# Softmax scaling and copies on another engine, weight conversion in whole pieces, and tables loaded elsewhere, in a fused attention, Fourier-mixing and feed-forward kernel

## The chip, the core and the metric

The kernel runs on one core of a Trainium2 chip. The core has five engines that each work through a list of instructions of their own, in order: TensorE (PE in the profile; PEld is its weight load), VectorE (DVE), ScalarE (ACT), GpSimd (POOL) and SyncE (SP), which here issues all the DMAs. The metric is the device time of one execution in microseconds. Before the change it is 2252.2 us, the median of three runs (2251.06 to 2255.11).

## What is computed

The reference is attention with normalised q and k, then a real part of a two-dimensional Fourier transform added to the result, then a normalised feed-forward block. There are 8 batches of 448 tokens, 12 heads of 64, so a model width of 768, and a hidden width of 3072. Everything is float32.

```python
rms = np.sqrt(np.mean(x * x, axis=-1, keepdims=True) + 1e-06)   # q and k: x / rms * g
scores = 1.0 / np.sqrt(64) * np.matmul(q_n, k_n.transpose(0, 1, 3, 2))
attn = np.exp(scores - np.max(scores, axis=-1, keepdims=True))
attn = attn / (np.sum(attn, axis=-1, keepdims=True) + 1e-09)
x = np.matmul(attn, v)                      # then heads side by side: (8, 448, 768)
mixed = np.real(np.fft.fft(np.fft.fft(x, axis=1), axis=2))
u = x + mixed
un = (u - mean(u)) / np.sqrt(var(u) + 1e-06)
out = u + np.maximum(un @ w_ch1, 0.0) @ w_ch2
```

The feed-forward weights come as float64 and are handed to the chip as pairs of 32-bit words.

## The kernel before

One batch goes through `attention`, `spectral` and `ffn`. The feed-forward part of batch b (`ffn(b)`) is interleaved by `merge` with attention and spectral part of batch b + 1 (`aux(b + 1)`), by costs that the generators yield. `aux(0)` has no feed-forward beside it: it is the start of the program. The code's order is a first wish; the compiler's scheduler then chooses the order on each engine from its own estimate, so what stands where is shown below from the built program.

**Attention** works on pairs of heads, six in a batch. `norm_pair` squares q and k, reduces to `ss`, raises to the power -0.5 on POOL (lines 239, `ss`), and multiplies; `gneg` is the product of the two norms' factors, loaded by `load_gains`. `transpose_pair` brings q and k into `QT` and `KD` (and `KL`, a remainder term). `softmax_pair` takes four row blocks c of 112 tokens: PE makes scores `S` for both heads, DVE takes the row extreme `mn`, ACT does the exponential into `P` and its row sum into `sm`, DVE adds 1e-9 to `sm` and takes the reciprocal, and then each half of `P` is scaled by it. In the first two batches (`EARLY = 2`) the first half is scaled on ACT and the second on DVE; later both are scaled on DVE. `value_pair` transposes `P` on PE into `pt`, copies it out to `T` and multiplies by v into `av`. In batch 0 (plain pairs, line 382) three of a pair's six copies `T` run on DVE and three on ACT. `fold` adds and subtracts halves of the attention output `xT` on DVE (`eo`, `sd`, `tot`).

**The spectral part** multiplies the folded halves by the tables `D1` and `D2` (`y`, `Y`, `ab`), which `load_dft` loads at the start, `D2` through a staging tile `d2s` of 113 rows that ACT copies and DVE subtracts from. Then it adds x (`u`), takes means and writes `u` to a DRAM buffer.

**The feed-forward part** has 24 `up` steps (18 matmuls into `h`, line 844) and 36 `down` steps (12 matmuls into `o`, line 865) per batch. Each product is three float32r passes with a high and a low part.

**Conversion.** In the first batch each of the 24 + 36 weight tiles is converted from 64-bit words by `convert` (line 632): a load into `dbl` (tag X, 4 slots), two ACT operations (lines 643, 644), three DVE operations (645, 649, 653), a POOL add (657), an ACT cast (658) and a POOL subtraction (659). A tile is done in two halves (line 688): 128x384 for a tile of w1, 128x256 for one of w2. The working tile `mag` (tag M) has two slots, each stream `W1`, `W2` three finished tiles. Converted tiles are also stored to DRAM, and later batches load them from there. `CONVERT_EARLY` spreads the first 14 tiles over `aux(0)`; names of those end in `e` (`magw1e`). The other 46 are converted during `ffn(0)`. `behind` ties each conversion instruction, during the start, to the fourth-last recorded one of its engine.

Most DVE, ACT and POOL work goes through a recording helper, so it shows line 111 (112 after the change); it is told apart by tile names.

Of the kernel before, what the change touches and what calls it, by code (L numbers as in the profile page):

```python
# [22 lines left out]
C = 112  # L23
# [64 lines left out]
def spectral_block(ctx, tc, q, k, v, g_q, g_k, w1, w2, d1, d2, out, nb=B):  # L88
# [54 lines left out]

    SLOTS = {"P": 8, "PT": 6, "X": 4, "M": 2, "unT": 6, "h": 6}

    def slot(tag, name, dtype=F32):
        return sb.tile([128, 900], dtype, tag=tag, name=name, bufs=SLOTS[tag])

    def sub(o, a, b_):
# [10 lines left out]

    KL = cpool.tile([128, 2, S], F32R, name="KL")
    G.memset(KL.bitcast(F32), 0.0)
# [162 lines left out]
    def softmax_pair(b, p, Pc):  # L325
        QT, KD, _ = ready[b, p]
        for c in range(NC):
            P = slot("P", f"P{b}_{p}_{c}")[:C, : 2 * S]
            Ph = [P[:, :S], P[:, S:]]
            mn = sb.tile([C, 2], F32, tag="mn", name=f"mn{b}_{p}_{c}", bufs=4)  # L330
            sm = sb.tile([C, 2], F32, tag="sm", name=f"sm{b}_{p}_{c}", bufs=4)
            cs = slice(c * C, (c + 1) * C)
# [34 lines left out]
            Pc.append(P)  # L367
            yield 760

    def value_pair(b, p, Pc, xT):  # L370
# [6 lines left out]
        if plain(b, p):  # L377
# [92 lines left out]
    rstds = {}  # L470

    def fold(b, p, xT, EO):

# [158 lines left out]
    def convert(src, bits, part, name):  # L632
# [30 lines left out]
    class Stream:  # L663
# [18 lines left out]
        def converted(self, i, name):  # L682
            hl = self.tile(name)
            src = self.doubles(i)
            bits = slot("M", f"mag{self.tag}{name}", U32)[:, : self.n * 128].rearrange(
                "r (c f) -> r c f", c=self.n
            )
            for c in (slice(0, self.n // 2), slice(self.n // 2, self.n)):
                convert(
                    src[:, c], bits[:, c], [hl[:, k, c] for k in range(2)],  # L690
                    f"{self.tag}{name}_{c.start}",
                )
            nc.sync.dma_start(self.kept(i), hl.bitcast(F32))
            return hl
# [205 lines left out]
    def warm():  # L900
# [45 lines left out]
```

## Time and profile before

| | before |
|---|---|
| median of the timed runs | 2252.2 us (2251.06 to 2255.11) |
| the profiled execution | 2245.9 us, span 2244.1 us |
| PE busy | 2107.8 us (94%) |
| DVE busy | 1636.7 us (73%) |
| ACT busy | 1074.1 us (48%) |
| POOL busy | 574.0 us (26%) |
| mean granted TensorE clock | 0.963 of full speed |

A share over the whole span is a mean over very different stages: in the first half millisecond of the span PE has gaps and the other engines are fuller, behind it PE has almost none. So the table by stage below is the one to start from. In all rows a time is in us unless it is marked as ns; the number in brackets behind a busy time counts instructions; what stands behind `<-` in square brackets is what ended the idle time ahead of an instruction. Durations of neighbouring instructions on one engine overlap a little, so the distance of two starts is what an instruction costs its engine in a row of them.

### The profile page before, as it was taken

How to read it: one execution, taken by the hardware profiler on the slowest of the kernel's cores; microseconds unless marked ns; L12 is line 12 of the kernel's file. 1: busy time of each engine (PE TensorE's matmuls, PEld its weight loads, DVE VectorE, ACT ScalarE, POOL GpSimd, SP SyncE). 2: the span in 40 equal slices, each digit the busy share in tenths (PEclk: the TensorE clock that was granted, in tenths of full speed). 3: DMA queues.
4: the chain of work that ended last, by engine and by line, in shares of the span. 5: the costliest groups of instructions: out<-in, count | busy, mean ns of one | idle time of the engine just before them, and what ended most of it. 6: DMA issues, size and time to landing. Idle time of an engine off the chain costs nothing.

```text
span 2244.1 us, 32060 instructions
## 1 busy us (share of the span) xinstructions
PE 2107.8 (94%) x11164; PEld 1851.1 (82%) x11164; DVE 1636.7 (73%) x3281; ACT 1074.1 (48%) x2452; POOL 574.0 (26%) x442
## 2 busy tenths in 40 slices
PE   6967986788999999999999999999999999999997
PEld 3336865667999999999999999999999999998997
DVE  6897899898688577876788587866788587753122
ACT  5856777475554255534554355524554355422100
POOL 5883567476122011210122021211121022000000
PEclk7997987899999999999999999999999999999999
DMA  5556555577755585556655575557655674539665
GB/s 137 174 167 210 171 171 163 173 266 256 218 174 169 184 238 165 180 182 207 200 171 177 193 222 169 173 177 225 187 171 177 207 215 161 177 132 279 212 215 136
DMA packets 299187, 425.37 MB, mean 190 GB/s; under 512 B 187489, under 2 KB 225362, under 8 KB 299026
## 3 DMA queue, kind: packets, MB, share of 16 engines
q1 hardware_dynamic: 299026, 423.32, 61.1%
q8 instruction: 89, 1.46, 0.3%
q14 instruction: 72, 0.59, 0.1%
HBM read 363.47 MB, written 65.27 MB: 191 GB/s over the span
## 4 chain that ended last, share of the span: by engine, by line
PE 76%; DVE 10%; issue 4%; DMA 3%; POOL 3%; ACT 2%; SPq 0%; DVEq 0%; POOLq 0%; ACTq 0%
PE h L844 28%; PE o L865 27%; PE S L342 5%; PE av L429 4%; PE pt L417 4%; PE y L520 1%; PE qk L305 1%; DVE magw L653 1%; DVE mn L111 1%; DMA dblw<-w 1%; POOL magw L657 1%; DVE magw L645 1%; PE oT L810 1%; DMA u_dram<-u 1%; DMA w<-w 1%
## 5 line engine op out<-in xcount | busy, mean ns | idle before, releaser
L865 PE MATMUL o<-hs,w 128*128 128x448 f32 x3456 | 801.0, 374 | 13.3 <-ACT w L658 4.4
L844 PE MATMUL h<-unT,w 128*128 128x448 f32 x3456 | 781.4, 371 | 3.3 <-DVE hs L111 3.3
L865 PEld LDWEIGHTS o<-hs,w 128*128 128x128 f32 x3456 | 643.9, 191 | 71.7 <-ACT w L658 5.8
L844 PEld LDWEIGHTS h<-unT,w 128*128 128x128 f32 x3456 | 640.5, 189 | 57.1 <-DVE hs L111 4.3
L111 ACT ACTIVATE P<-S,mn 112x448 f32<-112x448 f32 x384 | 243.1, 635 | 218.7 <-DVE mn L111 196.8
L111 POOL TENSOR_TENSOR qkn<-raw 112x1024 f32<-112x1024 f32 x47 | 90.4, 1924 | 740.4 <-PE qk L305 481.2
L111 DVE TENSOR_REDUCE mn<-S 112x1 f32<-112x448 f32 x384 | 232.9, 616 | 48.8 <-PE S L342 45.7
L111 ACT ACTIVATE hs<-h 128x448 fp32r<-128x448 f32 x192 | 104.4, 544 | 294.0 <-PE h L844 293.1
L111 DVE TENSOR_TENSOR acc<-o,acc 128x448 f32<-128x448 f32 x240 | 148.6, 620 | 106.9 <-PE o L865 105.2
L111 DVE SCALAR_TENSOR_TENSOR hs<-h,hs 128x448 fp32r<-128x448 f32 x192 | 119.2, 621 | 125.8 <-ACT hs L111 123.8
L429 PE MATMUL av<-T,vhl 128*128 128x448 f32 x504 | 181.5, 392 | 19.2 <-DVE T L111 12.5
L111 ACT CAST T<-pt 128x448 fp32r<-128x448 f32 x252 | 133.2, 532 | 133.9 <-PE pt L417 131.6
L111 DVE TENSOR_TENSOR T<-pt,T 128x448 fp32r<-128x448 f32 x252 | 154.9, 616 | 35.5 <-ACT T L111 34.0
L111 POOL TENSOR_TENSOR ss<-ss,nhalf 112x16 f32<-112x16 f32 x48 | 151.7, 3160 | 108.9 <-DVE ss L111 107.2
L111 DVE TENSOR_SCALAR P<-P,sm 112x448 f32<-112x448 f32 x336 | 159.5, 509 | 4.3
L342 PE MATMUL S<-KD,QT 128*112 128x448 f32 x352 | 142.6, 407 | 10.5 <-ACT P L111 5.2
L417 PE MATMUL pt<-ident,P 112*128 112x112 f32 x1008 | 147.0, 264 | 4.4 <-DVE R L111 2.8
L417 PEld LDWEIGHTS pt<-ident,P 112*128 112x128 f32 x1008 | 123.0, 143 | 25.7 <-DVE R L111 3.6
L111 POOL TENSOR_TENSOR rstd<-st,nhalf 112x1 f32<-112x1 f32 (+2 forms) x32 | 18.4, 575 | 487.5 <-DVE st L111 484.6
L342 PE MATMUL S<-KL,QT 128*112 128x448 f32 x352 | 134.7, 385 | 2.0 <-DVE KL L111 1.9
L429 PEld LDWEIGHTS av<-T,vhl 128*128 128x128 f32 x504 | 96.4, 192 | 32.0 <-DVE T L111 17.0
L657 POOL TENSOR_TENSOR magw<-magw,dblw 128x256 uint32<-128x256 uint32 (+1 forms) x92 | 87.4, 960 | 81.6 <-DVE magw L653 55.7
(121 smaller groups left out, 2680.3 us busy)
## 6 DMA issues: line engine op xcount, KB each, us to landing
w<-w SPq DMA_DIRECT2D x288, 512.0 KB, 4.3
w<-w SPq DMA_DIRECT2D x192, 768.0 KB, 4.5
dblw<-w SPq DMA_DIRECT2D x60, 256.0 KB, 3.0
dblw<-w SPq DMA_DIRECT2D x32, 384.0 KB, 3.9
raw<-q SPq DMA_DIRECT2D x96, 112.0 KB, 4.6
raw<-k SPq DMA_DIRECT2D x96, 112.0 KB, 3.7
v<-v SPq DMA_DIRECT2D x96, 96.0 KB, 3.6
u_dram<-u SPq DMA_DIRECT2D x24, 336.0 KB, 3.5
```

Source lines behind the costliest of these rows:

```text
L111: ins = emit(*args, **kwargs)
L305: nc.tensor.transpose(pt[:, c * C : (c + 1) * C], qk[:, i, c].rearrange("t h d -> t (h d)"), ident[:C, :C],)
L342: nc.tensor.matmul(s_, QT[:, h, cs], K[:, h], start=step == 0, stop=step == 1)
L417: nc.tensor.transpose(pt[:, c * C : (c + 1) * C], Pc[c][:, 512 * h + j * 128 : 512 * h + (j + 1) * 128], ident[:C, :C],)
L429: nc.tensor.matmul(av[:, :S], lv, T[:, i], start=(j == 0 and i == 0), stop=False)
L520: nc.tensor.matmul(o, src[:, par, t0 : t0 + n], D1[:, ri, par, cols], start=i != 1, stop=i != 0,)
L645: behind(nc.vector.tensor_scalar(out=value, in0=value, scalar1=MIN_HIGH, scalar2=MAX_HIGH, op0=ALU.max, op1=ALU.min,))
L653: behind(nc.vector.scalar_tensor_tensor(out=bits, in0=high, scalar=0xC0000000, in1=bits, op0=ALU.bitwise_and, op1=ALU.bitwise_or,))
L657: behind(nc.gpsimd.tensor_tensor(out=bits, in0=bits, in1=low, op=ALU.add))
L810: nc.tensor.transpose(op[:n, j * 128 : (j + 1) * 128], accs[b][:, 3 * half + j, t0 : t0 + n], ident,)
L844: pace(nc.tensor.matmul(o, w[:, a, c], unT[c][:, z], start=n == 0, stop=n == 17))
L865: pace(nc.tensor.matmul(o, w[:, a, f], hs[4 * g + f][:, z], start=n == 0, stop=n == 11))
```

## The change

Six things are edited.

1. In the first two batches both halves of `P` are scaled on ACT. In batch 0 the row sums of two row blocks are taken together (one addition and one reciprocal for four columns), in later batches those of all four (eight columns), and the scalings follow in a row.
2. In batch 0 all six copies `T` of a pair run on ACT.
3. `convert` takes a whole tile at once: 128x768 or 128x512. Tag X has two slots of double width. `fold` uses them in later batches.
4. `load_gains` stands ahead of the first pair's loads in the code.
5. `load_dft` is called at step 40 of `aux(0)` and no more after its first step; its second table comes in two DMAs, of 112 rows and of one row.
6. `KL` and `D2` share one tile, `rounded`.

```diff
     def softmax_pair(b, p, Pc):
         QT, KD, _ = ready[b, p]
+        together = 2 if b == 0 else NC
         for c in range(NC):
...
-            V.tensor_scalar(
-                out=sm, in0=sm, scalar1=1e-9, scalar2=None, op0=ALU.add
-            )
-            V.reciprocal(sm, sm)
-            for h in range(2):
-                if b < EARLY and h == 0:
-                    A.activation(Ph[h], Ph[h], AF.Copy, scale=sm[:, h : h + 1])
-                    continue
-                V.tensor_scalar(
-                    out=Ph[h], in0=Ph[h], scalar1=sm[:, h : h + 1], scalar2=None,
-                    op0=ALU.mult,
                 )
             Pc.append(P)
             yield 760
+            if (c + 1) % together:
+                continue
+            sums = sm[:, :together]
+            V.tensor_scalar(
+                out=sums, in0=sums, scalar1=1e-9, scalar2=None, op0=ALU.add
+            )
+            V.reciprocal(sums, sums)
+            for n, P in enumerate(Pc[c + 1 - together : c + 1]):
+                for h in range(2):
+                    ph = P[:, h * S : (h + 1) * S]
+                    if b < EARLY:
+                        A.activation(ph, ph, AF.Copy, scale=sums[:, n, h : h + 1])
+                    else:
+                        V.tensor_scalar(
+                            out=ph, in0=ph, scalar1=sums[:, n, h : h + 1], scalar2=None,
+                            op0=ALU.mult,
+                        )
...
-                    if (h * 3 + j) % 2 == 0:
-                        V.tensor_copy(T, pt[:, :S])
-                    else:
-                        A.copy(T, pt[:, :S])
+                    A.copy(T, pt[:, :S])
...
-        nc.sync.dma_start(st, d2.rearrange("s (n t) -> s n t", n=4))
+        for r in rows_of(N1):
+            nc.sync.dma_start(st[r], d2[r].rearrange("s (n t) -> s n t", n=4))
...
-            for c in (slice(0, self.n // 2), slice(self.n // 2, self.n)):
-                convert(
-                    src[:, c], bits[:, c], [hl[:, k, c] for k in range(2)],
-                    f"{self.tag}{name}_{c.start}",
-                )
+            convert(src, bits, [hl[:, k] for k in range(2)], f"{self.tag}{name}")
...
+    load_gains()
     load_pair(0, 0)
-    load_gains()
     warm()
-    side = aux(0)
-    next(side)
-    load_dft()
-    for _ in side:
-        convert_some(CONVERT_EARLY)
+    for n, _ in enumerate(aux(0)):
+        if n == DFT_STEP:
+            load_dft()
+        if n:
+            convert_some(CONVERT_EARLY)
```

The built programs show where these edits land. First DVE at the start of the program, before and after (`qkn`, `raw`, `ss`: the first pair's norms; `D_78`, `d2s`: the second spectral table and its staging tile).

```order
L903 MEMSET warm 128x512
L111 TENSOR_TENSOR qkn_0_137<-raw_0_110 112x1024
L111 SCALAR_TENSOR_TENSOR gneg<-gneg,gtmp 112x64
L111 TENSOR_REDUCE ss_0_139<-qkn_0_137 112x16
L111 TENSOR_TENSOR raw_0_110<-raw_0_110,gneg 112x512
L111 TENSOR_SCALAR ss_0_139<-ss_0_139 112x16
L111 TENSOR_TENSOR D_78<-d2s,D_78 113x4x113
L111 TENSOR_TENSOR qkn_0_137<-raw_0_110,ss_0_139 112x2x4x64 x2
```

```order
L917 MEMSET warm 128x512
L112 TENSOR_TENSOR qkn_0_136<-raw_0_112 112x1024
L112 SCALAR_TENSOR_TENSOR gneg<-gneg,gtmp 112x64
L112 TENSOR_REDUCE ss_0_138<-qkn_0_136 112x16
L112 TENSOR_TENSOR raw_0_112<-raw_0_112,gneg 112x512
L112 TENSOR_SCALAR ss_0_138<-ss_0_138 112x16
L112 TENSOR_TENSOR qkn_0_136<-raw_0_112,ss_0_138 112x2x4x64 x2
```

The subtraction on the table no longer stands ahead of the two multiplications into `qkn`; it comes some seventy rows later, behind the sums of pair 2. The rest is in the same order.

Then SP, its first DMAs, before and after (`gneg`, `gtmp`: the norms' factors; `dblw1e`: 64-bit weights to be converted).

```order
L205 DMA raw_0_110<-q 112x4x64 x2
L205 DMA raw_0_110<-k 112x4x64 x2
L174 DMA gneg<-g_q 112x64
L175 DMA gtmp<-g_k 112x64
L205 DMA raw_1_146<-q 112x4x64 x2
L205 DMA raw_1_146<-k 112x4x64 x2
L183 DMA d2s<-d 113x452
L640 DMA dblw1e_0_242<-w 128x3x256
L640 DMA dblw1e_3_252<-w 128x3x256
```

```order
L211 DMA raw_0_112<-q 112x4x64 x2
L211 DMA raw_0_112<-k 112x4x64 x2
L179 DMA gneg<-g_q 112x64
L180 DMA gtmp<-g_k 112x64
L211 DMA raw_1_145<-q 112x4x64 x2
L211 DMA raw_1_145<-k 112x4x64 x2
L658 DMA dblw1e_227<-w 128x6x256
L658 DMA dblw1e_293<-w 128x6x256
```

The factors' two DMAs stand where they stood, behind the first pair's q and k. The table's DMA is gone from here, and a weight tile is one DMA in place of two. The first table, `D1`, is in both programs issued between the loads of pair 2 and of pair 3.

Then ACT in pair 3 of batch 0, before and after (`P_3_1` is row block 1 of pair 3; a row that writes `P` and `sm` from `S` is an exponential, one that writes `P` from `P` and `sm` a scaling).

```order
L111 ACTIVATE P_3_0_733,sm_3_0_735<-S_3_0_0_736,mn_3_0_734 112x448
L111 ACTIVATE P_3_0_733,sm_3_0_735<-S_3_0_1_737,mn_3_0_734 112x448
L111 COPY T_2_0_1_807<-pt_2_0_1_802 128x448
L111 ACTIVATE P_3_1_787,sm_3_1_789<-S_3_1_0_790,mn_3_1_788 112x448
L111 ACTIVATE P_3_1_787,sm_3_1_789<-S_3_1_1_791,mn_3_1_788 112x448
L111 ACTIVATE P_3_0_733<-P_3_0_733,sm_3_0_735 112x448
L111 ACTIVATE P_3_2_839,sm_3_2_841<-S_3_2_0_842,mn_3_2_840 112x448
L111 COPY T_2_1_0_862<-pt_2_1_0_857 128x448
L658 CAST w2e_748<-magw2e_749 128x256
L111 ACTIVATE P_3_2_839,sm_3_2_841<-S_3_2_1_843,mn_3_2_840 112x448
```

```order
L112 ACTIVATE P_3_0_665,sm_3_0_667<-S_3_0_0_668,mn_3_0_666 112x448
L112 ACTIVATE P_3_0_665,sm_3_0_667<-S_3_0_1_669,mn_3_0_666 112x448
L112 COPY T_2_0_1_720<-pt_2_0_1_715 128x448
L112 ACTIVATE P_3_1_705,sm_3_0_667<-S_3_1_0_707,mn_3_1_706 112x448
L112 ACTIVATE P_3_1_705,sm_3_0_667<-S_3_1_1_708,mn_3_1_706 112x448
L112 COPY T_2_0_2_728<-pt_2_0_2_723 128x448
L112 ACTIVATE P_3_2_758,sm_3_2_760<-S_3_2_0_761,mn_3_2_759 112x448
L112 ACTIVATE P_3_0_665<-P_3_0_665,sm_3_0_667 112x448 x2
L112 ACTIVATE P_3_1_705<-P_3_1_705,sm_3_0_667 112x448 x2
L661 ACTIVATE magw2e_781<-dblw2e_782 128x512
L662 ACTIVATE dblw2e_782<-dblw2e_782 128x512
L676 CAST w2e_676<-magw2e_677 128x512
```

The scalings come four in a row behind the second row block's sums, and every copy `T` stands here.

Last ACT at the spectral part of batch 0, before and after (`Y` from `y`: the four casts that the product `ab` waits for; `dblw_6`: the load of a weight tile that `ffn(0)` uses).

```order
L111 COPY xr_0_1546<-xT_136 128x6x112
L111 COPY xr_0_1546<-xT_136 128x6
L658 CAST w1e_1379<-magw1e_1380 128x384 x2
L658 CAST w1e_1468<-magw1e_1469 128x384 x2
L111 CAST Y_0_0_1498<-y_0_0_1491 113x390
L644 ACTIVATE dblw_6_0_2205<-dblw_6_0_2205 128x256
L111 CAST Y_0_1_1508<-y_0_1_1501 112x390
L644 ACTIVATE dblw_6_2_2215<-dblw_6_2_2215 128x256
L111 CAST Y_1_0_1518<-y_1_0_1511 113x390
L111 CAST Y_1_1_1528<-y_1_1_1521 112x390
```

```order
L676 CAST w1e_1233<-magw1e_1234 128x768
L112 COPY xT_135<-av_5_1_1273 64x448
L112 COPY xT_135<-xT_135 128x1
L112 COPY xr_0_1380<-xT_135 128x6x112
L112 COPY xr_0_1380<-xT_135 128x6
L112 CAST Y_0_0_1332<-y_0_0_1325 113x390
L676 CAST w1e_1312<-magw1e_1313 128x768
L112 CAST Y_0_1_1342<-y_0_1_1335 112x390
L112 CAST Y_1_0_1352<-y_1_0_1345 113x390
L112 CAST Y_1_1_1362<-y_1_1_1355 112x390
L662 ACTIVATE dblw_6_2001<-dblw_6_2001 128x512
```

The operations on `dblw_6` stood between the casts of `Y`; now they stand behind all four, and one cast of a weight tile stands among them.

## Rows read from the trace of the kernel before

**Rows 1.** Busy time by stage: the stretch in us from the span's start, its length, then busy us of PE, PEld, DVE, ACT and POOL with instruction counts, the granted TensorE clock, the share of the DMA engines and GB/s.

```profile
0.00:50.00 50.00, 30.31 (x86) 16.27 (x86) 32.90 (x65) 25.41 (x58) 25.67 (x22) 0.73 0.45 123
50.00:140.00 90.00, 78.47 (x325) 32.13 (x323) 81.99 (x178) 75.17 (x194) 75.09 (x61) 0.98 0.57 169
140.00:200.00 60.00, 36.03 (x149) 24.40 (x150) 50.36 (x99) 31.39 (x69) 32.56 (x24) 0.69 0.66 204
200.00:400.00 200.00, 163.12 (x781) 136.87 (x780) 179.17 (x352) 147.00 (x350) 125.36 (x106) 0.86 0.55 173
400.00:560.00 160.00, 132.43 (x640) 114.21 (x640) 147.28 (x289) 92.22 (x223) 98.22 (x109) 0.91 0.69 234
560.00:2000.00 1440.00, 1439.90 (x8044) 1319.30 (x8043) 1081.95 (x2183) 671.58 (x1505) 214.89 (x119) 1.00 0.62 188
```

**Rows 2.** The timeline of the first 20 us, all engines: start, busy us, engine, line, operation, output and inputs, shapes.

```profile
5.85 0.39 SPq L183 DMA_DIRECT2D d2s<-d  x1
...
10.37 2.93 POOL L111 TENSOR_TENSOR ss<-ss,nhalf 112x16 f32<-112x16 f32 x1 [8.26 <-DVE ss L111]
...
17.66 0.57 ACT L111 CAST D<-d2s 113x452 fp32r<-113x452 f32 x1 [15.64 <-DMA d2s<-d]
...
18.80 1.28 DVE L111 TENSOR_TENSOR qkn<-raw,ss 112x512 f32<-112x512 f32 x2
```

**Rows 3.** Groups of DVE instructions from 50 to 140 us: count, busy us, mean ns of one, idle time ahead.

```profile
L111 DVE TENSOR_SCALAR P<-P,sm 112x448 f32<-112x448 f32 x20 | 15.0, 750 | 0.2
L111 DVE TENSOR_SCALAR sm<-sm 112x2 f32<-112x2 f32 x20 | 10.8, 541 | 0.0
L111 DVE COPY T<-pt 128x448 f32<-128x448 f32 x14 | 8.6, 614 | 3.6 <-PE pt L386 3.5
```

**Rows 4.** The same of ACT, from 50 to 140 us.

```profile
L111 ACT ACTIVATE P<-P,sm 112x448 f32<-112x448 f32 x20 | 13.4, 672 | 4.0 <-DVE sm L111 3.9
```

**Rows 5.** ACT's timeline around 70 to 76 us.

```profile
70.48 0.54 ACT L643 ACTIVATE magw1e<-dblw1e 128x384 f32<-128x384 f32 x1
70.93 0.54 ACT L644 ACTIVATE dblw1e<-dblw1e 128x384 uint32<-128x384 uint32 x1
...
74.87 0.68 ACT L111 ACTIVATE P<-P,sm 112x448 f32<-112x448 f32 x1
75.44 0.53 ACT L111 COPY T<-pt 128x448 f32<-128x448 f32 x1
75.85 0.54 ACT L111 COPY QT<-qk 128x448 f32<-128x448 f32 x1
```

**Rows 6.** Groups of DVE instructions from 200 to 520 us.

```profile
L111 DVE TENSOR_SCALAR P<-P,sm 112x448 f32<-112x448 f32 x28 | 21.4, 772 | 0.4
...
L111 DVE TENSOR_SCALAR sm<-sm 112x2 f32<-112x2 f32 x25 | 7.5, 301 | 3.3 <-ACT P L111 3.3
...
L111 DVE RECIPROCAL sm<-sm 112x2 f32<-112x2 f32 x25 | 3.9, 155 | 0.3
```

**Rows 7.** The timeline of 380 to 425 us, DVE and ACT.

```profile
382.27 0.45 DVE L111 TENSOR_SCALAR P<-P,sm 112x448 f32<-112x448 f32 x1
382.64 0.28 DVE L645 TENSOR_SCALAR magw<-magw 128x256 f32<-128x256 f32 x1
...
400.15 0.76 ACT L643 ACTIVATE magw<-dblw 128x256 f32<-128x256 f32 x2
...
400.82 0.50 DVE L645 TENSOR_SCALAR magw<-magw 128x256 f32<-128x256 f32 x2
...
422.95 0.35 DVE L645 TENSOR_SCALAR magw<-magw 128x384 f32<-128x384 f32 x1
```

**Rows 8.** PE's waits from 200 to 560 us: who waited for whom, us in total, times, longest.

```profile
PE av L429 <- DVE T L111: 12.5, 9, 3.3
...
PE o L865 <- ACT w L658: 4.4, 3, 2.8
```

**Rows 9.** The timeline of 167 to 173 us, ACT and PE at the spectral part of batch 0.

```profile
167.23 0.48 ACT L111 CAST Y<-y 113x390 fp32r<-113x390 f32 x1
...
170.70 0.43 ACT L644 ACTIVATE dblw<-dblw 128x256 uint32<-128x256 uint32 x1 [2.99 <-DMA dblw<-w]
171.03 0.47 ACT L111 CAST Y<-y 112x390 fp32r<-112x390 f32 x1
...
172.89 3.63 PE L593 MATMUL ab<-Y,D 112*113 112x390 f32 x9 [3.54 <-ACT Y L111]
```

**Rows 10.** DMA issues of the whole run, from the page: count, KB each, median us from issue to landing. `dblw` are 64-bit weights to be converted, `w` converted tiles.

```profile
w<-w SPq DMA_DIRECT2D x288, 512.0 KB, 4.3
w<-w SPq DMA_DIRECT2D x192, 768.0 KB, 4.5
dblw<-w SPq DMA_DIRECT2D x60, 256.0 KB, 3.0
dblw<-w SPq DMA_DIRECT2D x32, 384.0 KB, 3.9
```

**Rows 11.** The DMA queue's own waits from 200 to 540 us.

```profile
SPq L640 <- POOL magw L657: 118.0, 74, 6.8
```

**Rows 12.** Groups of POOL instructions from 200 to 520 us: the conversion's addition.

```profile
L657 POOL TENSOR_TENSOR magw<-magw,dblw 128x256 uint32<-128x256 uint32 x47 | 41.4, 891 | 30.3 <-DVE magw L653 19.5 <-issue 6.4 <-ACT P L111 3.6
...
L657 POOL TENSOR_TENSOR magw<-magw,dblw 128x384 uint32<-128x384 uint32 x32 | 36.3, 1143 | 39.0 <-DVE magw L653 29.4 <-DVE sm L111 5.2 <-issue 3.4
```

More of the change, by code (lines that the diff above doesn't have):

```diff
@@ L43 @@
 EARLY = 2
+DFT_STEP = 40
 PLAIN_PAIRS = range(NPAIR)
@@ L142, in bank, with wide @@
         return ps.tile([128, 512], F32, tag=tag, name=name, bufs=BANKS[tag])
-    SLOTS = {"P": 8, "PT": 6, "X": 4, "M": 2, "unT": 6, "h": 6}
+    SLOTS = {"P": 8, "PT": 6, "M": 2, "unT": 6, "h": 6}
     def slot(tag, name, dtype=F32):
         return sb.tile([128, 900], dtype, tag=tag, name=name, bufs=SLOTS[tag])
+    def wide(name, dtype=F32):
+        return sb.tile([128, 1800], dtype, tag="X", name=name, bufs=2)
     def sub(o, a, b_):
@@ L157, in rows_of @@
         return [slice(a, z) for a, z in ((0, n - n % 16), (n - n % 16, n)) if a < z]
-    KL = cpool.tile([128, 2, S], F32R, name="KL")
+    rounded = cpool.tile([128, 2 * S + 8 * N1], F32R, name="rounded")
+    KL = rounded[:, : 2 * S].rearrange("r (h t) -> r h t", h=2)
     G.memset(KL.bitcast(F32), 0.0)
@@ L169, in spectral_block @@
     D1 = cpool.tile([128, 2, 2, 5 * NI], F32, name="D1")
-    D2 = cpool.tile([N1, 2, 2, 2, N1], F32R, name="D2")
+    D2 = rounded[:N1, 2 * S :].rearrange("s (i c a t) -> s i c a t", i=2, c=2, a=2)
     u_dram = dram.tile([2, 4, N1, DM], F32, name="u_dram")
@@ L191, in spectral_block @@
     X_BANKS = (("either", "either"), ("either", "either"))
-    FOLD_SLOTS = (("unT", "unT"), ("PT", "P"), ("M", "X"))
+    FOLD_SLOTS = (("unT", "unT"), ("PT", "P"), ("M", None))
     loaded = {}
@@ L330, in softmax_pair @@
             mn = sb.tile([C, 2], F32, tag="mn", name=f"mn{b}_{p}_{c}", bufs=4)
-            sm = sb.tile([C, 2], F32, tag="sm", name=f"sm{b}_{p}_{c}", bufs=4)
+            if c % together == 0:
+                sm = sb.tile([C, NC, 2], F32, tag="sm", name=f"sm{b}_{p}_{c}", bufs=2)
             cs = slice(c * C, (c + 1) * C)
@@ L352, in softmax_pair @@
                     scale=-1.0,
-                    accum_out=sm[:, h : h + 1],
-                )
-            V.tensor_scalar(
-                out=sm, in0=sm, scalar1=1e-9, scalar2=None, op0=ALU.add
-            )
-            V.reciprocal(sm, sm)
-            for h in range(2):
-                if b < EARLY and h == 0:
-                    A.activation(Ph[h], Ph[h], AF.Copy, scale=sm[:, h : h + 1])
-                    continue
-                V.tensor_scalar(
-                    out=Ph[h], in0=Ph[h], scalar1=sm[:, h : h + 1], scalar2=None,
-                    op0=ALU.mult,
+                    accum_out=sm[:, c % together, h : h + 1],
                 )
@@ L470, in spectral_block @@
     rstds = {}
+    halves = {}
     def fold(b, p, xT, EO):
@@ L477, in fold @@
         once = slot(short, f"sd{b}_{p}").rearrange("r (i e t) -> r i e t", i=2, e=2)
-        eo = slot(kept, f"eo{b}_{p}").rearrange("r (i t) -> r i t", i=2)
+        if kept is not None:
+            eo = slot(kept, f"eo{b}_{p}")
+        else:
+            if p % 2 == 0:
+                halves[b] = wide(f"eo{b}_{p}")
+            eo = halves[b][:, p % 2 * 900 : p % 2 * 900 + 900]
+        eo = eo.rearrange("r (i t) -> r i t", i=2)
         add(eo[:, 0, :449], xT[:, p, :449], xT[:, p + 3, :449])
@@ L636, in convert @@
         _, c, f = src.shape
-        raw = slot("X", f"dbl{name}", U32)[:, : c * f].rearrange(
+        raw = wide(f"dbl{name}", U32)[:, : c * f].rearrange(
             "r (c f w) -> r c f w", c=c, w=2
@@ L687, in converted @@
             )
-            for c in (slice(0, self.n // 2), slice(self.n // 2, self.n)):
-                convert(
-                    src[:, c], bits[:, c], [hl[:, k, c] for k in range(2)],
-                    f"{self.tag}{name}_{c.start}",
-                )
+            convert(src, bits, [hl[:, k] for k in range(2)], f"{self.tag}{name}")
             nc.sync.dma_start(self.kept(i), hl.bitcast(F32))
```

## The prediction

> **What bounds the kernel now.** I read the busy times by stage first [rows 1]. From 560 to 2000 us PE is busy 1439.9 of 1440 us at full clock: what other engines gain there is worth nothing, and the changed program has the same matmuls. So the change can only pay before 560 us. From 50 to 140 us, the attention of batch 0, all engines are full, and DVE fullest: 82.0 of 90 us, against 78.5 on PE and 75.2 on ACT. From 200 to 560 us, the conversion beside the feed-forward of batch 0, PE is busy 163.1 + 132.4 = 295.6 of 360 us, so 64.4 us are idle, and DVE has 179.2 + 147.3 = 326.5 us (91%), ACT 239, POOL 224. The second view is PE's waits in that stretch [rows 8]: the longest sum, 12.5 us in 9 waits, is for a copy `T` from DVE; a weight from the conversion costs PE only 4.4 us. The third is the timeline of the start [rows 2]: ACT gets the table `d2s` 11.8 us after its issue (5.85 to 17.66), and DVE's multiplication into `qkn` starts at 18.80, though POOL's power was done at 10.37 + 2.93 = 13.30.
>
> **Start (edit 5).** The subtraction on the table no longer stands ahead of `qkn`, so `qkn` starts at about 13.4: 18.8 - 13.4 = 5.4 us earlier, and all behind it. Nothing else is late there: the power is the next thing waited for. Bounds: 0, if the later table costs as much where it now stands, and 5.5. I take 5.4, since ACT has its own queue of work ahead of the table's cast. That cast now needs a DMA that stands on SP behind the store of a converted tile. A 256 KB load lands in 3.0 us [rows 10]; if this one again took 11.8 us, ACT, and the copies and scalings behind the cast, could wait up to 8.8 us. I take nothing.
>
> Edit 4 doesn't do what it says: the scheduler leaves the factors' DMAs behind the first pair's q and k in both programs. It costs and gives nothing. Edit 6 neither: the table's part of the tile is written once, between matmuls that read the other part.
>
> **50 to 140 us (edits 1, 2, 3).** DVE loses 15.0 us of scalings, 14 copies for 8.6 us, half of the additions to `sm`, 5.4 us [rows 3]. With fewer reciprocals and conversion instructions that is some 32 us off 82, and DVE is no more the bound. ACT gets them. In a row of ACT instructions a scaling takes 0.57 us from start to start (74.87 to 75.44) and a copy 0.41 (75.44 to 75.85) [rows 5]. There were 20 scalings by ACT in this stretch [rows 4], and as many come: 20 x 0.57 = 11.4; 14 x 0.41 = 5.7. Whole pieces give some back: a half of 384 columns takes 0.45 us [rows 5], one of 256 columns 0.33 (two end after 0.76, the last lasts 0.43 [rows 7, 9]), so 128 columns cost 0.12, a whole tile of w1 about 0.81 for 0.90 and of w2 0.57 for 0.66: 0.09 for each of three operations on some nine tiles, 2.4 us. ACT then has 75.2 + 11.4 + 5.7 - 2.4 = 89.9 us of work in a stretch of 90. The bound has moved, and by as much as was freed. Bounds: nothing gained but 3 us, if these distances are 3% too long; 9 us lost, if ACT gets no fuller than DVE was (89.9 / 0.91 = 99). I take 3 us lost (97% full), because ACT's order here was made for it.
>
> **140 to 200 us (edits 2, 3).** At the spectral part ACT sat 2.99 us on the load `dblw`, with three casts of `Y` behind it; the second cast came at 171.03, the first at 167.23, and PE's `ab` at 172.89 waited 3.54 us for the last [rows 9]. In the new order all four stand ahead of that load: about 3.5 us. The last two DVE copies of pair 5 go too, 1.2 us at 0.6 each [rows 3]. Together 5 us gained; bounds 0 (the cast of a whole weight tile among them may come later by one POOL half, 1.1 us [rows 12], and the start of the stretch is ACT's now) and 8.
>
> **200 to 560 us (edits 1, 3).** Batch 1's 22 scalings in this stretch leave DVE: 22 x 0.772 = 17.0 us. Additions and reciprocals fall from four to one for a pair, some 17 less: 17 x (0.301 + 0.155) = 7.8 us [rows 6]. In 46 converted tiles each of three DVE operations is one instruction in place of two. Two of 256 columns take 0.50 us, one alone 0.28, one of 384 columns 0.35 [rows 7]; so 128 columns cost 0.07, the second half's 256 columns would add 0.14 in one instruction and add 0.22 in two. 0.08 x 3 x 46 = 11.0 us. Sum 35.8 us of 326.5, 11%. ACT gets 22 x 0.57 = 12.5 us and saves 46 x 3 x 0.09 = 12.4: no change, and it is 66% full. The wait that edit 1 adds, scalings only after all eight exponentials, holds back the pair's transposes on PE; behind it are feed-forward matmuls. If DVE were all, 250 to 560 us, where PE isn't full, would shrink with it: 39 us (35.8 / 0.91). If the conversion chain or ACT's waits take its place, 0. PE's idle time allows 64. I take 20, about the middle, since DVE is the fullest engine but only part of PE's waits name it.
>
> A scaling alone takes 0.45 us [rows 7] against the mean of 0.772 [rows 6], so part of what leaves is waiting beside POOL. The Trainium skill, page "SBUF — State Buffer", section "SBUF: two separate sides", says that DVE and GpSimd share a port pair that one instruction locks for its whole length. By that rule the wait may only pass to the next DVE instruction; with 22 x 0.45 the sum would be 28.7 in place of 35.8, and the 20 would be 16.
>
> **Behind 560 us.** From batch 2 on DVE does eight scalings in a row, 8 x 0.45 = 3.6 us, where products' results may wait. I take nothing: DVE has 25% of that stretch free [rows 1] and PE two banks for the products. If each of 36 pairs cost PE 0.5 us, 18 us would be lost.
>
> **Sum.** -5.4 + 3 - 5 - 20 = -27.4 us, on the profiled execution 2245.9 - 27.4 = 2218.5 us. The median shown is 6.3 us above that execution; from it, 2252.2 - 27.4 = 2224.8, so 2225.
>
> **Rivals.**
> DVE was the bound all through (chance 0.15): 39 us from 200 to 560 in place of 20, 8 in place of 5, no loss on ACT: 5.4 + 8 + 39 = 52, so 2200. For it speaks DVE's 91%; against, that ACT is as full in the first stage.
>
> The relief is hidden (0.16): behind ACT, the conversion's loads and waits in order, only the start and the casts stay: 2252.2 - 5.4 - 5 + 3 = 2245; with the later table waited for, no change. For it speaks that in batch 0 one full engine replaces another.
>
> The conversion chain becomes the bound (0.12), the slower side. With whole pieces a load can only start when the POOL addition on the whole tile is done: one half later, 0.89 us for w2 and 1.14 for w1 [rows 12]. It lands later, too: 4.3 against 3.0 us, 4.5 against 3.9 [rows 10]. That is 2.2 us for each of 30 tiles of w2 and 1.7 for 16 of w1, 93 us, and half of it with two slots: 47. Beside the forecast's other terms the time is 2225 + 47 = 2272. It decides from 27.4 / 46 = 0.6 us a tile that PE feels. For it: the queue stood 118.0 us in 74 waits for exactly that addition [rows 11]. Against: two halves of a tile already follow each other on each engine, and PE waited only 4.4 us for a finished weight [rows 8], three tiles being ahead. The Trainium skill, "Perfetto Trace Analysis", section "Optimizing Scalar/DVE Operations", has a rule for either side: larger operations where the engine is saturated, smaller ones where it isn't but causes bubbles elsewhere. DVE at 91% falls under the first; POOL at 224 of 360 us, which frees the slots, under the second, and by that one this rival's time holds.
>
> **How the numbers follow.** The forecast has 0.57, over gains of 12 to 40 us (the stage terms' bounds, not all at one end): 2212 to 2240. The range of 8 in 10 adds most of the first two rivals: 2203 to 2249. About 0.2%, 4.5 us, can be told from no change. Faster: 0.57 + 0.15 + 0.10 of the hidden case = 0.82; same 0.06 of it and 0.01; slower 0.11.
>
> **What would show it.** Right: `qkn` at 13 to 14 us; ACT over 95% and DVE under 65% busy in the pairs of batch 0, with pairs no closer than before; `Y` casts together; DVE under 85% and PE's idle time down by about 20 us before PE is full for good, and the period of a batch behind that unchanged. Wrong: ACT waiting longer for `dblw` and PE for `w`, new PE waits for `P` or `acc` behind 560 us, or `qkn` still behind something else.

## The result and the profile after

The changed kernel takes 2271.05 us (median of 4 runs, 2269.27 to 2274.02) against 2251.63 us before (4 runs, one more than the three of the table above, 2248.83 to 2255.11): ratio 1.0087, 95% interval 1.0069 to 1.0105. It is 19.4 us slower; 2225 was forecast. Its profiled execution took 2271.0 us, its median, with a span of 2269.1; the one of before (2245.9) lay 6 us under its own, so that stages compared between the two profiles look up to 6 us worse for the change than the medians do.

Busy time by stage in the changed kernel, columns as in [rows 1]:

```profile
50.00:140.00 90.00, 78.50 (x289) 30.62 (x287) 53.99 (x94) 80.22 (x183) 61.24 (x38) 0.91 0.50 151
140.00:200.00 60.00, 39.81 (x172) 26.76 (x172) 43.80 (x81) 36.46 (x72) 27.95 (x18) 0.72 0.58 183
200.00:400.00 200.00, 170.67 (x828) 145.79 (x827) 160.19 (x241) 155.09 (x316) 113.00 (x68) 0.90 0.57 184
400.00:560.00 160.00, 124.06 (x582) 105.95 (x581) 125.54 (x203) 80.77 (x145) 86.20 (x55) 0.87 0.65 223
560.00:2000.00 1440.00, 1425.17 (x7908) 1297.21 (x7907) 1067.49 (x1953) 662.51 (x1492) 217.99 (x119) 1.00 0.61 185
```

DVE got its relief: 160.19 + 125.54 = 285.7 us from 200 to 560, against 326.5 [rows 1]. PE gained nothing from it there: 294.7 us busy against 295.6. And behind 560 us, where PE idled for 0.1 of 1440 us, it now idles for 14.8. The spectral product `y` marks the batches there. Its first instructions of three batches in a row (start us, busy us):

```profile
1013.49 1.94 PE L538 MATMUL y<-D,eo 128*113 128x130 f32 x16
...
1265.17 1.94 PE L538 MATMUL y<-D,eo 128*113 128x130 f32 x16
...
1520.66 1.93 PE L538 MATMUL y<-D,eo 128*113 128x130 f32 x16
```

That is 251.7 and 255.5 us a batch; in the trace of before the same three stand 249.2 and 249.1 us apart:

```profile
1004.14 1.94 PE L520 MATMUL y<-D,eo 128*113 128x130 f32 x16
...
1253.33 1.94 PE L520 MATMUL y<-D,eo 128*113 128x130 f32 x16
...
1502.42 1.94 PE L520 MATMUL y<-D,eo 128*113 128x130 f32 x16
```

So the loss is in the part that I had left out of the sum. PE's waits from 560 to 2000 us (us in total, times, longest); before had none in this stretch. `hs` is the hidden layer that the products `o` read, one half made by ACT and one by DVE; `acc` collects `o`; `unT` is the input of `h`:

```profile
PE o L879 <- DVE acc L112: 4.0, 4, 1.3
PE o L879 <- DVE hs L112: 2.1, 2, 1.1
PE h L858 <- ACT unT L112: 1.8, 2, 0.9
PE h L858 <- DVE hs L112: 1.7, 5, 0.4
```

PE also does less while it counts as busy: its instructions overlap in the profile, and a short wait between two of them need leave no idle time. In the same 1440 us it runs 7908 matmuls in place of 8044 [rows 1], 136 fewer. At 1440 / 8044 = 0.18 us each that is, as an estimate, 24 us, of which 14.8 show as idle.

The place in one pair, DVE from 1130 us on:

```profile
1130.68 0.15 DVE L112 TENSOR_SCALAR sm<-sm 112x8 f32<-112x8 f32 x1
1130.91 0.62 DVE L112 TENSOR_TENSOR acc<-o,acc 128x448 f32<-128x448 f32 x1
1131.45 0.19 DVE L112 RECIPROCAL sm<-sm 112x8 f32<-112x8 f32 x1
1131.68 3.20 DVE L112 TENSOR_SCALAR P<-P,sm 112x448 f32<-112x448 f32 x2
1134.80 0.61 DVE L112 TENSOR_TENSOR rounded<-qk,KD 64x448 fp32r<-64x448 f32 x1
1135.34 2.25 DVE L112 TENSOR_SCALAR P<-P,sm 112x448 f32<-112x448 f32 x6
1137.51 1.21 DVE L112 TENSOR_REDUCE ss<-qkn 112x16 f32<-112x1024 f32 x1
1138.64 0.61 DVE L112 TENSOR_TENSOR acc<-o,acc 128x448 f32<-128x448 f32 x1
```

and PE, with POOL beside it:

```profile
1131.34 1.90 POOL L112 TENSOR_TENSOR qkn<-raw 112x1024 f32<-112x1024 f32 x1 [30.07 <-PE qk L311]
1133.32 1.32 POOL L112 TENSOR_TENSOR raw<-raw,gneg 112x512 f32<-112x512 f32 x1
...
1139.30 2.71 PE L879 MATMUL o<-hs,w 128*128 128x448 f32 x12 [0.64 <-DVE acc L112]
```

From 1131.68 to 1138.64 DVE adds nothing to `acc` and makes no `hs`, so it empties no bank of the feed-forward; the next product waits for its `acc`. The row lasts 5.9 us, where eight scalings undisturbed take 3.0 (shown below): one instruction on `rounded` stands in it, and its first two scalings end only when POOL's two multiplications have (1133.32 + 1.32 = 1134.64). The Trainium skill, page "SBUF — State Buffer", section "SBUF: two separate sides", says that whichever starts first, a GpSimd operation or a DVE operation of certain kinds, holds the port pair that both share for its whole length, and that the other is blocked. The trace agrees for these two multiplications. Beside POOL's power for `ss` no scaling was held up: in e5 a row of four takes 1.53 us from 691.52, inside a power that runs from 691.09 for 2.90 us.

### The profile page after: what moved, and what is told of

Read it like the earlier page. It is cut to its first block, busy times and chain, and to the rows that moved or that the text cites. A ratio compares the mean times of both kernels' runs of the same rounds, so it can differ in the third digit from the quotient of the medians.

```text
span 2269.1 us, 31138 instructions
## 1 busy us (share of the span) xinstructions
PE 2122.5 (94%) x11164; PEld 1853.7 (82%) x11164; DVE 1559.1 (69%) x2759; ACT 1082.7 (48%) x2338; POOL 535.9 (24%) x322
## 4 chain that ended last, share of the span: by engine, by line
PE 67%; DVE 12%; ACT 7%; DMA 7%; issue 4%; POOL 3%; SPq 0%; DVEq 0%; POOLq 0%; ACTq 0%
PE h L858 24%; PE o L879 24%; PE S L350 5%; PE av L439 4%; PE pt L427 4%; ACT P L112 3%; DMA w<-w 2%; DVE P L112 2%; DMA u_dram<-u 2%; DMA dblw<-w 1%; PE y L538 1%; POOL magw L675 1%; PE av L406 1%; PE qk L311 1%; DVE mn L112 1%
## 5 line engine op out<-in xcount | busy, mean ns | idle before, releaser
L879 PE MATMUL o<-hs,w 128*128 128x448 f32 x3456 | 789.0, 372 | 22.2 <-ACT w L676 7.0
L858 PE MATMUL h<-unT,w 128*128 128x448 f32 x3456 | 794.6, 374 | 9.5 <-DMA w<-w 3.2
L112 POOL TENSOR_TENSOR ss<-ss,nhalf 112x16 f32<-112x16 f32 x48 | 147.0, 3063 | 159.4 <-DVE ss L112 159.0
L439 PE MATMUL av<-T,vhl 128*128 128x448 f32 x504 | 176.0, 389 | 7.1 <-DVE T L112 2.9
L350 PE MATMUL S<-KD,QT 128*112 128x448 f32 x352 | 142.8, 407 | 17.8 <-ACT P L112 11.7
L427 PE MATMUL pt<-ident,P 112*128 112x112 f32 x1008 | 152.2, 262 | 5.6 <-DVE T L112 2.1
L112 DVE TENSOR_SCALAR P<-P,sm 112x448 f32<-112x448 f32 x288 | 148.1, 578 | 0.9
L350 PE MATMUL S<-rounded,QT 128*112 128x448 f32 x352 | 134.0, 382 | 0.6 <-DVE rounded L112 0.6
L675 POOL TENSOR_TENSOR magw<-magw,dblw 128x512 uint32<-128x512 uint32 (+1 forms) x46 | 72.3, 1571 | 77.9 <-DVE magw L671 59.2
```

The source lines that it names most:

```text
L112: ins = emit(*args, **kwargs)
L350: nc.tensor.matmul(s_, QT[:, h, cs], K[:, h], start=step == 0, stop=step == 1)
L427: nc.tensor.transpose(pt[:, c * C : (c + 1) * C], Pc[c][:, 512 * h + j * 128 : 512 * h + (j + 1) * 128], ident[:C, :C],)
L439: nc.tensor.matmul(av[:, :S], lv, T[:, i], start=(j == 0 and i == 0), stop=False)
L675: behind(nc.gpsimd.tensor_tensor(out=bits, in0=bits, in1=low, op=ALU.add))
L858: pace(nc.tensor.matmul(o, w[:, a, c], unT[c][:, z], start=n == 0, stop=n == 17))
```

## The experiments

Each ratio is against the kernel before on the same chip; that kernel's median was 2253.4 (e1 to e4), 2253.9 (e5, e7 to e9), 2253.4 (e6, e10, e12, e16), 2254.9 (e18, e19) and 2256.8 us (e21).

**Where the loss is.** e1 takes one piece of edit 1 back:

```diff
-        together = 2 if b == 0 else NC
+        together = (2, NC)[b] if b < EARLY else 1
```

> The changed kernel, but from batch 2 on each row block's sums are inverted and its two scalings issued at once, as before. Theory S (the loss is the wait for all eight sums and the eight scalings in a row, behind 560 us): the batch period goes from 254 back to 249 us, no PE wait for acc, hs or P is left between 700 and 2000 us, and 5 to 6 batches at 5 us come back: 2240 to 2250 us. Theory C (whole conversion pieces, with the fold's halves in one wide tile): 2265 to 2272 us, the period stays at 254.

2247.86 us, ratio 0.9966 (0.9951 to 0.9982). PE is full again behind 560 us:

```profile
560.00:2000.00 1440.00, 1439.25 (x8018) 1318.89 (x8018) 1082.12 (x2185) 671.57 (x1505) 214.51 (x120) 1.00 0.60 187
```

e2 adds the same piece alone to the kernel before.

> The kernel before, and of the change only the sums of four row blocks taken together from batch 2 on, with the eight scalings in a row on VectorE. Theory S: the whole loss of the steady part is there without any other edit, 2252 + 5 x 5.4 = 2279 us (2272 to 2285), the period 254. Theory C: 2250 to 2254 us, the period 249.

2273.47 us, ratio 1.0079 (1.0061 to 1.0097):

```profile
560.00:2000.00 1440.00, 1426.25 (x7894) 1295.95 (x7893) 1066.79 (x1953) 662.73 (x1492) 217.83 (x119) 1.00 0.60 185
```

Taken away the piece gives back 23 us, added it costs 20 (27 and 18 by the ratios). Theory S holds; with the piece gone PE idles for less than 1 us behind 560 us, so nothing else in the change costs time there.

e3 adds to the kernel before only edit 3 (the wide tiles, one `convert` a tile).

> The kernel before with whole conversion pieces alone (the wide tiles, and the fold's halves in one of them). Theory S: no loss behind 560 us; before it DVE loses 11 us of work and the time is 2240 to 2252 us. Theory C: 2265 to 2275 us, more SP time spent on the POOL addition and more PE waits for w.

2251.62 us, ratio 0.9988 (0.9975 to 1.0002): no difference shown. C falls as the cause of the loss.

e4 puts `load_dft()` back to the start of the changed kernel.

> The changed kernel with the tables loaded where they were before (ahead of the first pair's work). If the 5.4 us by which qkn starts earlier reach the end: 2276 us. If they are lost on the way to 560 us, behind ACT or behind the conversion: 2269 to 2273 us. Theories S and C both leave the period at 254.

2278.92 us, ratio 1.0101 (1.0082 to 1.0119), which overlaps the changed kernel's interval; the time is above both cases. But its profile corrects my picture of the start. SP, ACT and DVE:

```profile
5.84 0.86 SPq L189 DMA_DIRECT2D d2s<-d  x2
...
10.84 1.28 ACT L112 ACT_TABLE_LOAD   x1 [10.84 <-DMA d2s<-d]
12.14 0.57 ACT L112 CAST rounded<-d2s 113x452 fp32r<-113x452 f32 x1
...
13.79 1.29 DVE L112 TENSOR_TENSOR qkn<-raw,ss 112x512 f32<-112x512 f32 x2 [0.42 <-POOL ss L112]
```

Loaded first but in two pieces, 112 rows and one, the table has landed by 10.84 us (ACT's wait for it ends there; it then loads a table of its own before the cast), and `qkn` starts at 13.79; in the changed kernel it starts at 13.60, before at 18.80 [rows 2]. The pieces alone give the early start. The packets show how: the table's 113 packets of 1808 bytes run at most two at a time in the trace of before, for 8.9 us, and up to 16 at a time in e4, for 2.6 us.

**Eight in a row, or a late `P`?** e5 takes two row blocks together from batch 2 on (`together = NC if b == 1 else 2`).

> The changed kernel, but from batch 2 on the sums of two row blocks are taken together, with four scalings in a row in place of eight. With every scaling past the first two costing alike, a third of the loss of e1 against the changed kernel stays, (4 - 2) / (8 - 2) of 24 us: 2248 + 8 = 2256 us. If the work in flight covers 1.8 us but not 3.6 us: 2246 to 2250 us, no PE wait for P, acc or hs behind 700 us. If the wait for a later row's exponentials is what costs, not the length of the row: 2262 us or more.

2248.26 us, ratio 0.9963 (0.9950 to 0.9976), PE busy 1439.14: four in a row cost nothing. The price isn't even over the scalings.

Nor does every row of eight cost. Beside batch 2, from 580 to 730 us, PE runs as many matmuls in the changed kernel (first row) as before (second), and never idles:

```profile
580.00:730.00 150.00, 150.00 (x832) 137.10 (x831) 114.88 (x218) 77.26 (x176) 25.51 (x12) 1.00 0.58 179
580.00:730.00 150.00, 150.00 (x832) 136.67 (x831) 119.78 (x240) 77.75 (x176) 30.83 (x15) 1.00 0.57 175
```

The first of five rows of eight that begin there:

```profile
590.70 2.99 DVE L112 TENSOR_SCALAR P<-P,sm 112x448 f32<-112x448 f32 x8
```

Four of the five take 2.98 to 2.99 us, one 3.52. Of the 30 rows of batches 3 to 7, 21 take 4.5 to 6.4 us, drawn out by other DVE instructions between the scalings and by POOL's multiplications, which 24 of the 30 meet. PE's first idle time of over 0.1 us comes behind the first of these (0.27 us at 821; the row takes 4.54 us from 814.80). So the changed kernel loses where its rows are drawn out to 4.5 us and more, and nothing is seen to be lost where they take 3.0. The rows of four in e5 take 1.5 us, at most 2.1, and none is drawn out by POOL's multiplications: e5 doesn't tell a shorter row from an undisturbed one, and no run keeps the eight scalings and moves POOL's work away.

e10 is e1 with dead work behind each pair's last scalings:

```diff
+            if b >= EARLY and c == NC - 1:
+                extra = sb.tile([C, 5], F32, tag="extra", name=f"extra{b}_{p}", bufs=1)
+                for n in range(5):
+                    V.tensor_reduce(
+                        extra[:, n : n + 1], P[:, S:], axis=AX.X, op=ALU.min
+                    )
```

> e1 (sums by row from batch 2 on) with five more VectorE instructions, reductions over the scaled last row of a pair that nothing uses, in a row behind its scalings: 5 x 0.55 = 2.75 us, as long as the six scalings that stand in the longer row of the changed kernel, but here P isn't late. Theory D (the loss is that VectorE is blocked, and acc, hs and mn stand behind the row): 2265 to 2275 us, with PE waits for acc and hs behind 700 us. Theory P (the loss is that the scaled P comes late for PE's transposes): 2246 to 2251 us, no such waits. If both have a part, the time lies between, and its share of the 24 us is that of D.

2270.19 us, ratio 1.0068 (1.0049 to 1.0086): 22 us above e1. `P` isn't late here (its scalings stand as in e1, and PE has no wait for a `P` of DVE behind 560 us), and PE loses as much:

```profile
560.00:2000.00 1440.00, 1425.70 (x7906) 1299.77 (x7905) 1164.96 (x2338) 668.12 (x1493) 214.22 (x121) 1.00 0.61 185
```

So a VectorE blocked by a row is enough for a loss of that size, though it is only 81% busy (74% in the changed kernel). e6 moves all eight scalings to ScalarE (`if b < nb:`).

> The changed kernel with all eight scalings on ScalarE in every batch, so that VectorE has no row of them, but P comes even later, 8 x 0.57 = 4.6 us behind the last exponential. Theory D: 2246 to 2254 us, the period 249 to 250. Theory P: 2272 us or more, PE waiting at rem and pt. If ScalarE's own row blocks its hs and T: 2260 us or more, with PE waits for hs and T on ACT.

2267.64 us, ratio 1.0055 (1.0033 to 1.0076). The loss stays: PE's largest wait is now for `hs`, whose first half ScalarE makes, 3.8 us in 4 (the profile names DVE, which makes the second). The third case of the expectation holds for the time and for `hs`; a wait for `T` on ACT doesn't show. A row that long hurts on either engine; whether a late `P` has a part here isn't shown.

**Where the first 560 us went.** e7 is e1 with the conversion in halves.

> e1 (the changed kernel with sums by row from batch 2 on) with the conversion in halves again. Theory H (ahead of 560 us the end of batch 1's chain, not the conversion, sets the time): 2245 to 2251 us, as e1. If whole pieces give DVE relief that reaches PE: 2255 or more. If whole pieces hold the weights back, and so ate the gain of edit 1: 2230 to 2240 us.

2240.64 us, ratio 0.9928 (0.9916 to 0.9941), the fastest of all and 7 us below e1. The last case holds, 0.6 us outside its range. From 460 to 560 us, where the conversion paces PE, e1 and then e7 have

```profile
L879 PE MATMUL o<-hs,w 128*128 128x448 f32 x163 | 40.5, 400 | 6.4 <-POOL w L677 4.4 <-DVE hs L112 0.8 <-ACT w L676 0.6
L858 PE MATMUL h<-unT,w 128*128 128x448 f32 x126 | 29.3, 391 | 0.1
```

```profile
L875 PE MATMUL o<-hs,w 128*128 128x448 f32 x156 | 37.1, 383 | 7.8 <-POOL w L669 2.1 <-DVE hs L112 1.7 <-ACT hs L112 1.5
L854 PE MATMUL h<-unT,w 128*128 128x448 f32 x159 | 36.8, 382 | 3.3 <-DVE hs L112 3.3
```

289 products against 315. Beside the other edits whole pieces hold the weights back.

e8 folds batch 1's first two pairs within the loop (`if p > 3:`).

> e1, but batch 1 folds its pairs 0 and 1 within its loop over pairs, as all other batches do, and not all three at its end. Theory H (the lead that PE has at 400 us is lost in its 15 us wait for the folds' eo): that wait falls below 8 us and the time is 2236 to 2243 us. If the conversion or ACT's work is what sets the pace from 400 to 560 us: 2246 to 2250 us, with the 8 us or more turned into waits for w. If the extra tile that each fold holds makes the pairs wait for P: 2250 us or more.

2248.18 us, ratio 0.9968 (0.9954 to 0.9981), as e1. The changed kernel waits 15.6 us for `eo` from 200 to 560 us, the longest single wait. Here it is gone and nothing is won: from 460 to 560 us 277 products, with waits for `w` in its place. Theory H falls for whole pieces.

e9 puts the moved work back on VectorE, sums by row everywhere.

> The changed kernel with the work that edits 1 and 2 take off VectorE put back (second scalings and every other copy on VectorE, sums by row in all batches); whole pieces and the later tables stay. If the relief is hidden: 2245 to 2250 us, as e1. If it is worth the 20 us I forecast and something else ate it: 2262 us or more. If ACT's added work costs more than it gives: 2235 to 2243 us.

2256.99 us, ratio 1.0012 (0.9999 to 1.0025): the relief, with its merged sums, is worth 9 us here, less than the 20. The time fits none of the three cases.

e16 is the whole change with halves.

> The changed kernel with the conversion in halves and all else kept. If whole pieces cost the same beside the eight scalings in a row: 2272 - 7.6 = 2264 us (2260 to 2267). If the end of batch 1's chain hides it in this order: 2270 to 2274.

2268.97 us, ratio 1.0065 (1.0046 to 1.0084), overlapping the changed kernel's; inconclusive. e12 is the try for the best:

> e7 (sums by row from batch 2 on, halves), with sums of two rows in all batches and batch 1's first two folds within its loop. If the 16.9 us wait for eo now bounds, since the weights no longer do: 2228 to 2236 us. If it stays hidden, as with whole pieces: 2238 to 2243 us.

2242.63 us, ratio 0.9944 (0.9926 to 0.9963), no better than e7; the wait for `eo` is 7.4 us. e18 (e7 with the tables first) and e19 (e7 with the moved work back on VectorE) make a table of two by two with the kernel before and e7, though not a clean one, since e18 keeps the table's two pieces and with them the early start:

> e7 (halves, sums by row from batch 2 on) with the tables loaded first again, so of the change only the work that moves from VectorE to ScalarE in batches 0 and 1. If the start and the relief add up, with 5.4 us for the start and some 8 us for the relief (e7 stands 13 us below the kernel before): 2246 us. If the relief only pays because qkn starts earlier, or the start only because DVE has room: 2251 to 2255 us.

> e7 with the relief undone (second scalings and every other copy on VectorE, sums by row everywhere), so of the change only the later tables. If the start and the relief add up: 2253.5 - 5.4 = 2248 us. If the 5.4 us at the start are lost in the 50 to 140 us behind it, where all engines are full: 2252 to 2255 us, and then the relief is worth all 13 us of e7.

e18: 2256.44 us, ratio 1.0004 (0.9990 to 1.0018). e19: 2244.89 us, ratio 0.9961 (0.9949 to 0.9974). They don't add up: nothing and 9 us alone, 16 together by the ratios; e18 is 1 us above its second case, and e19 3 us below its first. And the start can't be the reason: in e18 `qkn` starts at 14.63 us, 0.9 us behind e7. Later tables help by something that I haven't found; its price between e18 and e7, 16 us, isn't what e4 shows (under 8). In the profiles the granted clock differs as well: 0.67 in e18 and 0.74 in e7 from 140 to 200 us, 0.86 and 0.89 from 200 to 400, some 10 us of full clock as an estimate (0.07 x 60 + 0.03 x 200). Whether that is cause or consequence isn't shown, and the profiled execution of e18 is its slowest (2260.56).

e21 is e7 with each row's scalings at once in all batches.

> e7 with each row block's sums and scalings in all batches at once and ahead of the next steps, as before, so of the change the later tables and the work moved to ScalarE stay. In e7 batch 0's spectral part begins at 173 us against 156 in the kernel before. If that comes from the sums taken for two (batch 0) and four (batch 1) rows: it begins at 150 to 160 us, and the time is 2230 to 2237 us. If it comes from ScalarE being full: 168 us or later, and 2238 to 2243 us.

2252.21 us, ratio 0.9982 (0.9970 to 0.9994). The spectral part of batch 0, at 156.28 us before and 165.56 after, begins at 179.93 here. So it isn't the merged sums that delay it. The time fits neither case: it is some 12 us above e7, and that is what the merged sums of batches 0 and 1 are worth there, together with one more difference: e21 also puts the later batches' scalings ahead of the next steps, as before.

## Why the prediction was wrong

**Behind 560 us: the step that failed.** I counted the eight scalings, wrote down their price (0.5 us a pair, 18 us), and took nothing, because DVE has 25% free and PE two banks. The measured price is 2271.05 - 2247.86 = 23.2 us (e1), 0.64 us for each of 36 pairs. The free quarter was no cover: with PE at 99.99%, what counts is how long its next result or operand has to wait. The length of the row was wrong, too. By [rows 7] a scaling in a row costs 0.37 us from start to start (382.27 to 382.64), so that eight take 3.0 us and not 3.6, and such rows cost nothing in batch 2; but from batch 3 on most rows take 4.5 to 6.4 us, 5.9 in the one shown, where they meet POOL and other DVE work. I had the wait beside POOL in the 200 to 560 us stage and not here. In e10 2 scalings and 5 reductions, 0.8 + 2.7 us by themselves, weren't covered either. The named sign, new PE waits for `P` and `acc`, is what the profile shows, with more for `hs`; that the two full banks are what holds PE up fits the waits for `acc`, and is argued, not shown.

The Trainium skill, page "Perfetto Trace Analysis", section "Optimizing Scalar/DVE Operations", has both halves of this: larger operations where the engine is saturated, broken-up ones where ScalarE or VectorE isn't but makes others wait. I used it for the conversion only, and there for POOL, of which the section doesn't speak. The runs agree with it on the sums: made one larger operation, with the scalings in a row behind it, they pay in batches 0 and 1 (e7 against e21, as far as that pair goes), and cost 23 us where DVE is 74% busy and PE full.

**Start.** `qkn` starts at 13.60 us, 13.4 forecast. But I gave the credit to the order; e4 shows that the split does it. The 113 rows in one DMA were the cost: 11.8 us, against 5.0 in two pieces in e4 and 7.1 in e18 (5.84 to its cast at 12.94). The Trainium skill, page "DMA: Bandwidth & Descriptors", section "Why a DMA increments its semaphore by 16 and not by 1", says that a transfer is spread over the largest count up to 16 that divides its outer dimension, so that by it 113 rows use one engine and 112 rows sixteen. The times agree with it, and so do the packets: at most two at a time before, up to 16 in e4.

**50 to 140 us.** The direction was right, the size not. DVE fell to 53.99 us, ACT rose to 80.22 of 90, short of the 97%. PE's waits for `T` changed engine, from 9.7 us, most of it on DVE (two rows of before), to 7.9 us on ACT (third row, changed kernel):

```profile
PE av L396 <- DVE T L111: 7.1, 4, 2.4
PE av L396 <- ACT T L111: 2.6, 2, 1.7
PE av L406 <- ACT T L112: 7.9, 7, 2.1
```

With batch 0's spectral part 9.3 us later in spite of a start 5.2 us earlier, some 14.5 us are lost on the way, where I took 3 (bound 9). That ACT's added work loses them isn't shown, and two runs speak against it. The part begins as late in e9 (first row), which has that work back on VectorE, and in e3 (second), which has only the whole pieces:

```profile
165.63 3.68 PE L541 MATMUL y<-D,eo 128*113 128x130 f32 x16 [4.25 <-DVE eo L112]
...
167.74 3.81 PE L531 MATMUL y<-D,eo 128*113 128x130 f32 x16 [7.03 <-DVE eo L111]
```

In e19, with neither, it begins at 173.48. (One execution fixes the place to some 5 us: e1, e5, e6 and e10 have the changed kernel's first batch and begin at 169 to 171 us.) What the profiles do show is a slower PE. Its granted clock from 50 to 140 us is 0.91 in place of 0.98, and it is as busy, 78.50 and 78.47 us, for 289 matmuls as for 325 before. Most of that lies between 63 and 77 us, in the changed kernel (first row) at half clock, 1.2 in place of 2.4 GHz:

```profile
63.00:77.00 14.00, 14.00 (x29) 4.83 (x30) 8.60 (x13) 13.51 (x31) 8.30 (x6) 0.51 0.47 141
63.00:77.00 14.00, 12.96 (x52) 4.92 (x48) 13.97 (x34) 12.45 (x33) 11.10 (x8) 1.00 0.51 146
```

In the 13 us ahead of the fall PE was busy for 8.85. By 90 x (0.98 - 0.91) the clock takes some 6 us, an estimate. It isn't all: in e9 the clock is 0.96, and the part begins as late. ACT is busy for 13.5 of those 14 us as well; what begins the delay stays open.

**140 to 200 us.** Right, and more than forecast: `ab` waits 0.17 us in place of 4.19 and 3.54:

```profile
173.78 1.69 PE L611 MATMUL ab<-Y,rounded 112*113 112x390 f32 x8 [0.17 <-DVE Y L112]
```

From `y` to the first `h` it takes 194.91 - 165.56 = 29.4 us; before, 156.28 to 196.37, 40.1. That is 10.7 us won, 5 forecast, and it pays for most of what was lost ahead of it.

**200 to 560 us.** DVE's relief was forecast well (35.8 us, measured 40.8), its worth not: 20 taken. PE's waits there are

```profile
PE y L538 <- DVE eo L112: 15.6, 1, 15.6
PE S L350 <- ACT P L112: 10.1, 5, 4.4
PE o L879 <- ACT w L676: 7.0, 5, 3.9
...
PE av L439 <- DVE T L112: 2.9, 6, 1.2
```

The 12.5 us for `T` [rows 8] went, as I had said, and others came in their place. What all edits but the late sums are worth is e1's 5.6 us, near the second rival's 7. Whole pieces take about 7 away from it (e7), 0.16 us for each of 46 tiles where the third rival had 1.0; that they do it by that rival's mechanism fits the waits for `w`. Sum, with the late sums as e2 measured them by themselves: -5.6 + 20.1 = 14.5 us; measured 19.4. By the ratios it is -7.7 + 17.8 = 10 against 19.6. Each of the three ratios has an interval of some 4 us to either side, so the two parts may add up or cost a few us more together.

So the forecast's sign was wrong by one term set to nothing, and its size by 20 us for a relief of which little reached PE. The rival that ended near the time (2272) did so for another reason, by luck.

**What stays open.** Why the later tables are worth so much more beside the relief (e18 against e7) than `qkn` explains. Why the whole pieces cost 7 us beside the other edits and nothing alone (e3). The moved work isn't needed for it: without it, beside the later tables, they cost 12 us (e9 against e19, 1.0012 and 0.9961). So what whole pieces cost hangs on the tables' place or pieces. No run has a third wide tile, which would let loads start earlier. Early and late part of the change should have been judged apart: e7 keeps the early one without whole pieces, and beats both kernels.

## What to carry to other kernels

When PE is full, look at the longest row of instructions on the engine that empties its banks, not at that engine's busy share, and at what draws the row out: here rows of 1.5 us were free, rows of 3.0 us undisturbed cost nothing that shows, and 23 us were lost where most took 4.5 to 6.4 us. The same merging can pay in another stage, so set it by stage, as e7 does. When an expected gain is worked out from one engine's relief, name the next two waits in that stage and take the gain only up to them.

## What the runs showed of the hardware

A table of 113 rows took 11.8 us as one DMA, with at most two packets at a time; as 112 rows and one it landed 5.0 us after the first issue, with up to 16 at a time. Two scalings of 0.45 us took 3.20 us beside two POOL multiplications, and ended within 0.3 us of the second; beside POOL's power four of them took 1.53 us, as undisturbed ones do. At a granted clock of half, 14 us of PE held 29 matmuls where they held 52 before.

And a group's sum of busy time says nothing of waits by itself: the 120 matmuls into `rem` from 760 to 2000 us, at a mean of 259 to 260 ns, sum to 18.6 us before, 24.7 after and 26.3 in e6, since 77, 37 and 30 of them stand directly behind another and overlap with it.
